# Turning the PSUM banks of the plain blocks by one and making exp(q) one block sooner, in a fused linear-attention and SiLU-MLP kernel

## The chip, the cores and the metric

The kernel runs on one core of a Trainium2 chip. The metric is the device time of a run in microseconds (us), lower is better. A core has five engines that work side by side: PE multiplies matrices and writes its results to PSUM, which has eight banks; ACT evaluates functions such as exp, tanh and silu; DVE and POOL do elementwise work and sums; SP issues most transfers. Only ACT and DVE take results out of PSUM here, so a bank that PE has filled can be filled again only when one of them has read it.

## The reference, cut to what matters

```python
q_s = exp(q - max(q));  q_s = q_s / sum(q_s, over the head dimension)
k_s = exp(k - max(k));  k_s = k_s / sum(k_s, over the sequence)
kv  = k_s^T v                      # per batch and head, 64 x 64
x   = q_s kv                       # reordered to 4608 tokens x 512
out = silu(x @ w_in) @ w_out       # w_in 512 x 2048, w_out 2048 x 512
```

There are 8 batches of 576 rows. The kernel cuts the 4608 tokens into 9 chunks of 512 (0 to 8). It overlaps three things: the first product and the silu of chunk t, the second product of chunk t-1, and the attention of the batch that chunk t+1 needs.

## The kernel before: the parts concerned

Part of the first product is done by seven-multiplication block recursion. In a chunk, half of it comes as 8 **plain blocks** (`p`, one PSUM bank each) and half as 7 **groups** (`g`, two banks each); 14 half-products of the second product (`b`) lie between them. One order is common to chunks 2 to 7:

```python
mix = "pbpbpbpbpbpbpbp", "ggbgbgbgbbgbgb"     # chunk 8 has the second half first
ps_ = [
    lambda t=t, i=i, fb=fb: mm1(t, fb, i < 4 or t + 1 >= B)
    for i, fb in enumerate((0, 8, 1, 9, 2, 10, 3, 11))
]
```

So block 0 is followed by a half-product, and so on, and after block 7 come group 1 and group 2 back to back. The banks of the plain blocks come from a counter (`hb[0]`) taken modulo the length of a ring (`hb[1]`), those of the groups are fixed:

```python
def mm1(t, fb, one=False):
    bank = hb[0] % hb[1]
    hb[0] += 1
    mm1_mm(t, fb, bank, range(NC))                      # 4 matmuls, line 274
    if one:
        nc.scalar.activation(..., func=ACT.Silu, ...)   # line 291: ACT frees the bank
    else:
        mm1_silu(t, fb, bank)      # tanh on ACT (246), then (1 + tanh) * h on DVE (247)

def group(t, i):
    bank = 0 if i in (1, 6, 7, 4) else 2
    ...
    for p in range(4):
        for c in range(2):
            nc.tensor.matmul(out=PS[:, bank + p // 2, ...], ...)    # line 362
```

Tanh and exp come from one ACT table, silu from another. Blocks whose last argument is true use silu; the others use tanh, so that exp(q) can run among them without another table. With tanh the bank is free only after DVE's half. In chunk t the preparation of the next batch is planned at places counted from the chunk's begin `u` (block i is at place 2i):

```python
plan(begin[2], lambda: (hb.__setitem__(0, 3), hb.__setitem__(1, 4)))
plan(begin[3], lambda: hb.__setitem__(0, 1))
...
plan(u + 7 + i, lambda i=i, b=b: exp_q(b, i))
plan(u + 8 + 2 * i, lambda i=i, b=b: (qsum(b, i), qnorm(b, i, nc.gpsimd)))
```

`qsum` is a row sum and a reciprocal on DVE (lines 144 and 148), `qnorm` a multiplication on POOL (line 153). After the last chunk 14 closing half-products (line 460) follow; the first of them writes bank 3.

Three more lines of DVE are named below. Line 480 adds what a product has left in PSUM to a copy that ACT made earlier; the addition called "sa" reads the bank that product 5 writes next. Line 341 adds banks 2 and 3 of a group to a copy that ACT made of banks 0 and 1; group 5 writes bank 2 next. Line 434 makes sums and differences for the second product.

The softmax here doesn't subtract the row's maximum and nothing guards it: scores larger than these inputs give would overflow.

## Time and profile before

| | before |
|---|---|
| time, median of the first 3 runs | 279.14 us (278.73 to 279.38) |
| span of the profiled execution | 277.5 us |
| PE busy | 260.6 us |
| chunk 3 to chunk 4, start of the first group | 28.95 us |
| of it PE waiting ahead of the group | 1.96 us |

The page gives busy time as an average over the span. The last two rows come from the timeline of PE and say more, because a chunk repeats: what is lost in one chunk is lost four times. The lines that carry this are shown in the prediction.

### The profile page before, as it was taken

To read this page: it belongs to the slowest core of one execution; us is meant where nothing else is said; L and a number is where in the kernel's file an instruction comes from. 1 tells how busy PE (TensorE), PEld (TensorE's weight loads), DVE (VectorE), ACT (ScalarE), POOL (GpSimd) and SP (SyncE) were. 2 spreads that over 40 slices of the span, in tenths; PEclk is the share of its full clock that TensorE was granted. 3 is DMA by queue.
4 is the path that set the end of the run, shared out by engine and by line. 5 is a ranking of instruction groups with operands and counts; after the bars stand their busy time and mean duration, and the time that the engine had idled before them with its cause. 6 is when DMAs were issued, how large, how long until landed. Compare 5 with 4: busy or idle time off the path is not lost.

```text
span 277.5 us, 6052 instructions
## 1 busy us (share of the span) xinstructions
PE 260.6 (94%) x2539; PEld 184.7 (67%) x2540; DVE 186.2 (67%) x264; ACT 179.0 (64%) x228; POOL 70.7 (25%) x62
## 2 busy tenths in 40 slices
PE   8799999999999997999799979997999999999993
PEld 3467644456678765876587658764876587886783
DVE  2867797979698749584858495768667237944533
ACT  5667936678866884787568756876677436574310
POOL 1744970900190009000910073005500000000003
PEclk9999999999999999999999999999999999999998
DMA  7999999499369716961696359740406002400534
GB/s 247 322 201 366 260 328 340 119 304 375 108 167 338 165 57 181 328 158 40 191 298 189 73 170 246 241 94 0 87 21 133 0 2 48 106 0 2 123 69 115
DMA packets 35500, 45.88 MB, mean 165 GB/s; under 512 B 16208, under 2 KB 20048, under 8 KB 35472
## 3 DMA queue, kind: packets, MB, share of 16 engines
q1 hardware_dynamic: 29568, 33.69, 43.0%
q0 software_dynamic: 5584, 11.54, 15.9%
q8 instruction: 20, 0.33, 0.5%
q10 hardware_dynamic: 320, 0.26, 0.3%
q14 instruction: 8, 0.07, 0.1%
HBM read 36.70 MB, written 9.44 MB: 166 GB/s over the span
## 4 chain that ended last, share of the span: by engine, by line
PE 71%; DVE 13%; ACT 7%; DMA 4%; issue 2%; SPq 1%; POOL 1%; DVEq 0%
PE PS L460 29%; PE PS L274 16%; PE PS L362 16%; DVE zq L144 5%; DVE GT L247 4%; DMA vt<-in_v_dram 4%; PE PS L398 3%; PE PS L254 3%; ACT eq L108 3%; PE PS L185 2%; ACT L108 2%; PE PS L224 2%; DVE rzq L148 1%; SPq L97 1%; DVE eq L153 1%
## 5 line engine op out<-in xcount | busy, mean ns | idle before, releaser
L274 PE MATMUL PS<-XT,W 128*128 128x512 f16 (+1 forms) x288 | 71.2, 373 | 0.3 <-ACT ow L410 0.3
L460 PEld LDWEIGHTS <-GT 128*128 128x128 f16 x512 | 49.6, 98 | 13.0 <-issue 1.2
L153 POOL TENSOR_TENSOR eq<-eq,rzq 128x1152 bf16<-128x1152 bf16 x13 | 27.5, 2117 | 111.6 <-DVE rzq L148 111.5
L460 PE MATMUL PS<-W,GT 128*128 128x256 f16 x384 | 49.1, 273 | 0.0
L460 PEld LDWEIGHTS <-S 128*128 128x128 f16 x384 | 37.6, 98 | 8.8
L274 PEld LDWEIGHTS <-W 128*128 128x128 f16 x288 | 27.9, 98 | 21.3 <-issue 1.3
L341 DVE TENSOR_TENSOR h<-PS,h 128x1024 f32<-128x1024 f32 x21 | 25.7, 1224 | 24.4 <-ACT h L338 15.3
L247 DVE SCALAR_TENSOR_TENSOR GT<-sg,PS 128x512 f16<-128x512 f32 (+2 forms) x52 | 33.5, 669 | 10.1 <-ACT sg L246 9.8
L246 ACT ACTIVATE sg<-PS 128x512 f32<-128x512 f32 (+2 forms) x52 | 30.1, 596 | 13.4 <-PE PS L274 9.1
L338 ACT COPY h<-PS 128x1024 f32<-128x1024 f32 x21 | 21.3, 1012 | 24.7 <-PE PS L362 24.7
L291 ACT ACTIVATE GT<-PS 128x512 f16<-128x512 f32 x36 | 21.4, 595 | 19.0 <-PE PS L274 18.4
L460 PE MATMUL PS<-T,S 128*128 128x256 f16 x256 | 32.7, 273 | 0.0
L362 PEld LDWEIGHTS <-W 128*128 128x128 f16 x168 | 16.4, 97 | 13.0 <-issue 10.5
L362 PEld LDWEIGHTS <-WS 128*128 128x128 f16 x224 | 21.0, 98 | 4.3 <-issue 1.8
L144 DVE TENSOR_REDUCE zq<-eq 128x18 f32<-128x1152 bf16 x12 | 16.2, 1347 | 11.2 <-ACT eq L108 11.2
L362 PE MATMUL PS<-XS,WS 128*128 128x256 f16 x168 | 21.8, 273 | 0.4 <-ACT h L338 0.4
L362 PE MATMUL PS<-XT,W 128*128 128x256 f16 x112 | 13.7, 272 | 8.5 <-DVE GT L247 7.8
L684 POOL DMA_DIRECT2D out_dram<-ow x4 | 2.2, 550 | 73.4 <-DVE ow L669 73.4
L347 ACT ACTIVATE GT<-h 128x1024 f16<-128x1024 f32 x21 | 20.7, 1052 | 0.0
L111 ACT ACTIVATE ek<-kt 128x1152 bf16<-128x1152 f32 x16 | 18.6, 1164 | 1.8 <-DMA kt<-in_k_dram 1.8
L108 ACT ACTIVATE eq<-qt 128x1152 bf16<-128x1152 f32 x16 | 18.1, 1158 | 2.5 <-DMA qt<-in_q_dram 2.4
L91 POOL CAST vaug<-vt 128x1152 bf16<-128x1152 f32 x12 | 19.4, 1648 | 0.0
(78 smaller groups left out, 337.5 us busy)
## 6 DMA issues: line engine op xcount, KB each, us to landing
out_dram<-ow SPq DMA_DIRECT2D x64, 128.0 KB, 2.4
qt<-in_q_dram SPq DMA_DIRECT2D x12, 576.0 KB, 4.7
kt<-in_k_dram SPq DMA_DIRECT2D x12, 576.0 KB, 7.1
vt<-in_v_dram SPq DMA_DIRECT2D x12, 576.0 KB, 6.1
qt<-in_q_dram POOLq DMA_DIRECT2D x4, 576.0 KB, 13.0
kt<-in_k_dram POOLq DMA_DIRECT2D x4, 576.0 KB, 13.2
vt<-in_v_dram POOLq DMA_DIRECT2D x4, 576.0 KB, 12.5
W<-in_moe_w_out_dram POOLq DMA_DIRECT2D x4, 512.0 KB, 15.2
```

Of the source, the lines that this page charges most:

```text
L108: nc.scalar.activation(out=half(st[b]["eq"], cc), in_=jgd(b, "qt", cc), func=ACT.Exp)
L144: nc.vector.reduce_sum(out=z, in_=e, axis=AX.X)
L153: eng.tensor_tensor(out=e, in0=e, in1=r[:, :, :, None].to_broadcast([128, J, 2, D]), op=ALU.mult)
L246: nc.scalar.activation(out=s, in_=i, func=ACT.Tanh, scale=OS)
L247: nc.vector.scalar_tensor_tensor(out=o, in0=s, scalar=1.0, in1=i, op0=ALU.add, op1=ALU.mult)
L274: nc.tensor.matmul(out=PS[:, bank, o0:TCH], lhsT=W1[:, c, fb * 128:(fb + 1) * 128], rhs=XTS[t % 2][:, c, o0:TCH], start=(c == 0), stop=(c ...
L291: nc.scalar.activation(out=GTS[t % 2][:, fb, 0:TCH], in_=PS[:, bank, :], func=ACT.Silu, scale=1.0 / XS)
L338: nc.scalar.copy(out=H[i], in_=PS[:, 0:2, :].rearrange("p b n -> p (b n)"))
L341: nc.vector.tensor_tensor(out=H[i], in0=PS[:, 2:4, :].rearrange("p b n -> p (b n)"), in1=H[i], op=ALU.add)
L347: nc.scalar.activation(out=group_out(t, f, n), in_=x, func=ACT.Silu, scale=1.0 / XS)
L362: nc.tensor.matmul(out=PS[:, bank + p // 2, (p % 2) * HT:(p % 2 + 1) * HT], lhsT=a[:, c, p * 128:(p + 1) * 128], rhs=bb[:, c, :], start=(i ...
L460: nc.tensor.matmul(out=PS[:, bank, m * HN:(m + 1) * HN], lhsT=a[:, fc, m * 128:(m + 1) * 128], rhs=bb[:, fc, :], start=(first and fc == 0) ...
```

## The change

The intent, as the change states it: the plain blocks' banks are turned by one so that the last two blocks lie in the pair of banks that the groups fill second, and exp(q) is made two blocks sooner, with the second row sum behind a later block. (By the edit it is two places, 7 to 5, which is one block: exp follows block 2's silu where it followed block 3's.)

```diff
-            lambda t=t, i=i, fb=fb: mm1(t, fb, i < 4 or t + 1 >= B)
+            lambda t=t, i=i, fb=fb: mm1(t, fb, i < 3 or t + 1 >= B)
...
-    plan(begin[2], lambda: (hb.__setitem__(0, 3), hb.__setitem__(1, 4)))
-    plan(begin[3], lambda: hb.__setitem__(0, 1))
+    plan(begin[2], lambda: (hb.__setitem__(0, 0), hb.__setitem__(1, 4)))
...
-                plan(u + 7 + i, lambda i=i, b=b: exp_q(b, i))
-                plan(u + 8 + 2 * i, lambda i=i, b=b: (qsum(b, i), qnorm(b, i, nc.gpsimd)))
-                plan(u + 12 + 2 * i, lambda i=i, b=b: vcast(b, i, nc.gpsimd))
+                plan(u + 5 + i, lambda i=i, b=b: exp_q(b, i))
+                plan(u + 6 + 3 * i, lambda i=i, b=b: (qsum(b, i), qnorm(b, i, nc.gpsimd)))
+                plan(u + 10 + 2 * i, lambda i=i, b=b: vcast(b, i, nc.gpsimd))
...
-                    plan(u + 9 + i, lambda i=i, b=b: load(b + 1, "qt", q, i, nc.sync))
+                    plan(u + 7 + i, lambda i=i, b=b: load(b + 1, "qt", q, i, nc.sync))
...
-            plan(u + 14, lambda b=b: q_transpose(b))
+            plan(u + 13, lambda b=b: q_transpose(b))
```

| block | 0 | 1 | 2 | 3 | 4 | 5 | 6 | 7 |
|---|---|---|---|---|---|---|---|---|
| bank before (chunks 3 to 8) | 1 | 2 | 3 | 0 | 1 | 2 | 3 | 0 |
| bank after | 0 | 1 | 2 | 3 | 0 | 1 | 2 | 3 |

## The prediction

> **What bounds the kernel now.** I read the page first. PE is busy for 94% of the span; no other engine passes 67%.
>
> ```profile
> PE 260.6 (94%) x2539; PEld 184.7 (67%) x2540; DVE 186.2 (67%) x264; ACT 179.0 (64%) x228; POOL 70.7 (25%) x62
> ...
> PE 71%; DVE 13%; ACT 7%; DMA 4%; issue 2%; SPq 1%; POOL 1%; DVEq 0%
> ```
>
> PE carries 71% of the chain that ended last, but DVE and ACT stand in it with 20%: there PE stood still. The waits of PE alone say where:
>
> ```profile
> PE PS L362 <- DVE GT L247: 7.8, 5, 1.8
> ...
> PE PS L362 <- ACT GT L291: 0.7, 1, 0.7
> ```
>
> L362 is the first product of a group, L247 the DVE half of a block's silu. The wait comes once in each token chunk of 512 that has a group behind plain blocks (chunks 2 to 7): about 1.8 us in chunks 3 to 6, 0.58 in chunk 2, 0.7 in chunk 7, where silu is one ACT instruction. Everything else PE waits for in the steady part is 0.4 us. The chain around one wait (chunk 4; start, length, what):
>
> ```profile
> 126.64 0.88 PE PS L274 x4
> 127.51 0.02 issue
> 127.53 0.04 ACT GT L291
> 127.58 0.57 issue
> 128.15 1.14 ACT L108
> 129.29 0.16 issue
> 129.44 1.17 ACT eq L108
> 130.62 0.02 issue
> 130.64 1.36 DVE zq L144
> 132.00 0.03 issue
> 132.03 0.02 DVEq L148
> 132.05 0.04 issue
> 132.10 0.27 DVE rzq L148
> 132.36 0.54 DVE GT L247
> 132.91 1.27 DVE zq L144
> 134.17 0.02 issue
> 134.20 0.27 DVE rzq L148
> 134.46 1.74 DVE GT L247 x3
> 136.21 0.04 issue
> 136.25 1.91 PE PS L362 x16
> ```
>
> Read it from the top: block 3 ends on PE, ACT does its silu, loads another table, makes exp(q); DVE makes two row sums, each ahead of silu halves that are waiting, and only then frees the last block's bank. PE's last block, in the timeline, starts at 133.42 and takes 0.87, so PE is free at 134.29 and starts the group at 136.25: **1.96 us idle per chunk**. The chunk lasts 28.95 us (107.30 to 136.25 between group starts), so its PE work is 26.99.
>
> The banks explain why it waits for the *last* block. Before, from chunk 3 on, blocks 0..7 lie in banks 1,2,3,0,1,2,3,0; group 1 fills banks 0 and 1, group 2 banks 2 and 3. The first matmul of group 1 goes to bank 0, which holds block 7. In chunk 2 they lie in 3,0,1,2,3,0,1,2, which is why that wait is short.
>
> **What the Trainium skill says.** "PSUM — Partial Sum Buffer", in its summary for kernel authors, says to guard PSUM by bank and to read one bank while the matmul targets another. The trace agrees: group 1 starts 0.04 us after the last L247 in its bank. "ScalarE: Activation LUTs", section "What ACT_TABLE_LOAD costs", gives about 1283 ns for the load plus about 1380 ns of drain. The trace has five loads of 1.28 us at L108; no such drain is visible (silu ends 128.13, load 128.15, exp 129.44). The same page lists exp and tanh in one set: the trace has no load between exp and tanh here. "SBUF — State Buffer", section "Who interferes with whom", says that DVE instructions with two SBUF inputs contend with GpSimd reads. The trace agrees: the L434 subtraction that follows the last silu takes 1.69 us beside POOL's work in chunk 4, and 1.22 in chunk 7 without it.
>
> **The change part by part.** The order of instructions per engine shows: PE, POOL and SP keep their order. ACT keeps its 173 rows; its table load and two exps move ahead by one silu, and block 3 becomes tanh. DVE gets five more rows (one L247 in each of chunks 2 to 6): about 0.6 x 5 = 3 us of DVE work, on an engine with a third idle. The first row sum comes ahead of block 3's half, the second behind block 4's; the addition "sa" moves between.
>
> *Turned banks.* Blocks now lie in 0,1,2,3,0,1,2,3. Group 1 needs blocks 4 and 5, group 2 blocks 6 and 7. The order's waits show four on DVE, one per bank, each four matmuls (half of 0.87 = 0.44 us) apart. So the group starts at once and needs the last bank only 1.31 us later.
>
> *exp(q) sooner.* Block 2's silu ends at 126.40 (start 125.80, 0.60). I move the ACT chain by 1.73, the distance of two blocks' silus (127.53 - 125.80):
> - exp 127.71 to 129.93 for both; tanh of blocks 3, 4, 5 at 129.84, 130.31 and 131.00 (5 by its matmuls' end); tanh 6 at 132.74 and 7 at 134.48, both still bound by PE; 7 ends 135.08.
> - DVE: first sum at 128.91, reciprocal 130.37, block 3's half 130.55, "sa" 131.09, block 4 at 131.7, second sum 132.25 (1.38 to its reciprocal), block 5 at 133.8 to 134.43, block 6 to 135.0, block 7 from 135.12 to 135.75.
>
> Put together, PE free at 134.29: bank 0 is free (block 4 ended about 132.3), bank 1 asked for at 134.73 (free 134.47), bank 2 at 135.16 (free 135.04), bank 3 at 135.60, free at 135.79. **Left over: 0.19 us instead of 1.96, a gain of 1.77**, four times: 7.1 us.
>
> *Chunk 2.* Before: PE free 77.30, the product after the two groups at 80.09; two groups take 1.74, so 1.05 idle. After, as above, 0.19. Gain 0.86.
>
> *Chunk 7* (no exp, all silu on ACT): free 221.11, started 221.95. Block 7's silu ends at 221.91; its bank is now asked for only at 222.42. Gain 0.84.
>
> *Chunk 8, a loss.* Here groups come first, and the closing products follow the plain blocks at once: the first goes to bank 3. Before, bank 3 held block 6 and nothing waited. Now it holds block 7, whose silu runs 261.07 to 261.67. The products started at 260.87; they will start at about 261.71. Loss 0.84, in a run of products that is the chain to the end.
>
> Sum: 7.1 + 0.86 + 0.84 - 0.84 = 7.9 us; 279.14 - 7.9 = **271.2 us**, 2.8% less. Each part alone, by the same clockwork: banks alone gain about 1.3 a chunk (block 7 still at 136.20, its bank needed last), earlier exp alone 0.46 (136.25 to 135.79).
>
> **The rivals.**
> (1) *A new wait takes its place inside the group.* PE gains 1.77 us but DVE only 0.45, so DVE runs 1.3 us later against PE. I checked each consumer: product 5 overwrites the bank that "sa" reads: needed 132.54, ready 131.78 (margin 0.76). The L434 result for product 7: needed 137.96, ready 137.35 (0.6). Group 5 overwrites bank 2, read by the L341 addition: needed 138.84, ready about 138.5 (0.3). The first is paid by moving "sa" behind a 1.36 us row sum. For it: margins are small, and POOL slows DVE. Against it: before, DVE idled 0.56 and 2.20 us in that stretch, so it catches up. If group 5 waits 0.3 in five chunks: 272.7.
> (2) *The preparation of q, k and v becomes the bound:* POOL's normalisations and casts, the transpose, exp(k). POOL starts its second normalisation about 0.5 earlier while PE runs 1.77 earlier; casts end about 139.4, k-v products want them at 140.68 (margin 1.2). The transposed q is wanted at 143.3 and lands near 140.7 (136.1 + 4.6). Little speaks for it; it would give back up to 1 us a chunk, 276.
> (3) *The gain is only that of the earlier exp* because group 1 waits as a whole for its pair and the next: then 0.63 stays per chunk and the result is 273.5. The waits per bank speak against it.
> (4) *The end's loss is hidden:* then 270.4. The products there run without a gap to the last, so I don't expect it.
>
> **How the range and the chances follow.** The sum of the measured times gives 271.2. Rival 1 makes it 272.7, rival 4 270.4; the three runs before spread 0.65 us. I take 270.2 to 273.0. Two per cent would be 273.56, which needs 2.4 us of the 7.9 to fail in the recurring chunks; I give 0.9 to faster, 0.09 to same, 0.01 to slower.
>
> **What would show it.** Right: the waits of PE for L247 at L362 shrink from 7.8 to about 1 us in all, in pieces near 0.2; chunks of the steady part last about 27.2 us; exp starts about 1.73 us sooner against its chunk; DVE has five more L247 and ACT five fewer L291; a new wait of about 0.7 to 0.8 us of the closing products (L460) for ACT's L291. Wrong: a wait at L362 for L341, at L460 for L434 or L480, or at the k-v products for POOL or ACT; or group 1 still starting late after block 7.

## The result, and the profile after

The changed kernel took 271.18 us (median of 4, 270.92 to 271.64) against 278.94 (median of 4) for the kernel before, 7.76 us less. The ratio is 0.9723, 95% interval 0.9702 to 0.9744. A ratio here is the mean time of one kernel's fast runs over that of the other's fast runs of the same rounds, so it is not quite the ratio of the two medians.

On the page of the changed kernel (the profiler's summary of one execution), the busy times and the chain by engine. The chain is the work that ended last, followed back at each step to what released it:

```profile
PE 260.4 (97%) x2540; PEld 184.6 (69%) x2540; DVE 190.6 (71%) x269; ACT 180.1 (67%) x228; POOL 71.1 (26%) x62
...
PE 71%; DVE 15%; ACT 8%; issue 3%; DMA 1%; POOL 1%; DVEq 0%
```

PE does the same 260 us of work in a shorter span, and DVE has five more instructions. The chain still passes through DVE and ACT with about the same share. That alone would look as if nothing had changed: the chain follows whatever released PE last, and DVE still releases the group last, however short the wait. How long PE stood still is in the list of its waits (engine, line, waited for: us in total, times, longest), of which these are the ones of the chunks and of the end:

```profile
PE PS L460 <- ACT GT L291: 0.7, 1, 0.7
PE PS L362 <- ACT h L338: 0.4, 1, 0.4
```

The 7.8 us of line 362 waiting for line 247 and the 0.7 waiting for line 291 are gone from the list, and one new wait of 0.7 us is there: the closing products, as predicted. The list is not the whole truth, though. Here is PE's timeline around the groups of chunk 4 before (start, length, engine, line; idle before in brackets):

```profile
133.42 1.03 PE L274 MATMUL PS<-XT,W 128*128 128x512 f16 x4
136.25 1.91 PE L362 MATMUL PS<-XT,W 128*128 128x256 f16 x16 [1.80 <-DVE GT L247]
137.99 1.04 PE L460 MATMUL PS<-T,S 128*128 128x256 f16 x8
```

And the same place after:

```profile
130.40 1.03 PE L274 MATMUL PS<-XT,W 128*128 128x512 f16 x4
131.26 2.17 PE L362 MATMUL PS<-XT,W 128*128 128x256 f16 x16
133.26 1.04 PE L460 MATMUL PS<-T,S 128*128 128x256 f16 x8
```

After the change the group starts 0.86 us after block 7, which is the time of the block itself: at once. But from its start to the next product are 2.00 us, where 1.74 are work. The missing 0.26 us is a wait inside the group, and only the start-to-start distance shows it. The chain of waits of the changed kernel at this place (start, length, what) says for what:

```profile
130.90 0.56 DVE GT L247
131.46 0.01 issue
131.46 0.61 ACT sg L246
132.07 0.02 issue
132.09 0.70 DVE GT L247
132.79 0.04 issue
132.83 0.60 PE PS L362 x4
```

The last four of the group's 16 matmuls, those in bank 3, start 0.04 us after DVE's half of block 7, and that half follows block 7's own tanh. The row sums are no longer directly ahead of it. The chain names DVE as what released that tanh, but it was PE. What ended on DVE at 131.46 is block 5's half, and in chunk 4 before, block 7's tanh began (134.48) while block 5's half was still running (134.38 to 135.01). In both traces the tanh starts 1.06 us after block 7's first matmul (130.40 to 131.46, 133.42 to 134.48).

At the end, PE's timeline from the last plain block, first before, then after:

```profile
260.01 1.03 PE L274 MATMUL PS<-XT,W 128*128 128x512 f16 x4
260.87 3.66 PE L460 MATMUL PS<-W,GT 128*128 128x256 f16 x32
```

```profile
251.02 1.03 PE L274 MATMUL PS<-XT,W 128*128 128x512 f16 x4
252.73 3.65 PE L460 MATMUL PS<-W,GT 128*128 128x256 f16 x32 [0.69 <-ACT GT L291]
```

From block to product 0.86 us have become 1.71: a loss of 0.85 that the change itself brought in.

Where the time came from, by the starts in the timelines of the two profiled executions:

| stretch | before | after | gain |
|---|---|---|---|
| start to block 1 of chunk 2 | 66.01 | 65.50 | 0.51, code unchanged |
| chunk 2, block 1 to the product behind the groups | 14.08 | 13.28 | 0.80 |
| chunks 3 to 6, block 0 of chunk 3 to block 0 of chunk 7 | 115.78 | 108.94 | 6.84 (4 x 1.71) |
| chunk 7, block 0 to group 1 of chunk 8 | 26.98 | 26.14 | 0.84 |
| chunk 8, group 1 to the closing products | 25.80 | 26.65 | -0.85 |

The parts that the change touches sum to 7.63 us; the runs show 7.76. The two spans differ by 8.1, because the profiled execution of the changed kernel also had the shorter start.

### The profile page after: what moved, and what is told of

Its sections match the earlier page's. It is cut to its first block, busy times and chain, and to the rows that moved or that the text cites. A ratio compares the mean times of both kernels' runs of the same rounds, so it can differ in the third digit from the quotient of the medians.

```text
span 269.4 us, 6058 instructions
## 1 busy us (share of the span) xinstructions
PE 260.4 (97%) x2540; PEld 184.6 (69%) x2540; DVE 190.6 (71%) x269; ACT 180.1 (67%) x228; POOL 71.1 (26%) x62
## 4 chain that ended last, share of the span: by engine, by line
PE 71%; DVE 15%; ACT 8%; issue 3%; DMA 1%; POOL 1%; DVEq 0%
PE PS L460 29%; PE PS L274 16%; PE PS L362 14%; DVE zq L144 5%; DVE GT L247 4%; PE PS L398 3%; PE PS L254 3%; ACT eq L108 3%; PE PS L224 2%; PE PS L185 2%; DVE eq L153 2%; ACT sg L246 2%; ACT L108 2%; DMA qt<-in_q_dram 1%; DVE ow L480 1%
## 5 line engine op out<-in xcount | busy, mean ns | idle before, releaser
L247 DVE SCALAR_TENSOR_TENSOR GT<-sg,PS 128x512 f16<-128x512 f32 (+2 forms) x57 | 37.4, 671 | 10.4 <-ACT sg L246 9.7
L246 ACT ACTIVATE sg<-PS 128x512 f32<-128x512 f32 (+2 forms) x57 | 33.1, 595 | 16.9 <-PE PS L274 8.1
L291 ACT ACTIVATE GT<-PS 128x512 f16<-128x512 f32 x31 | 18.5, 595 | 13.3 <-PE PS L274 12.7
L254 PE MATMUL PS<-XT,W 128*128 128x288 f16 x128 | 16.5, 286 | 0.7 <-DVE GT L247 0.4
```

The source lines that it names most:

```text
L246: nc.scalar.activation(out=s, in_=i, func=ACT.Tanh, scale=OS)
L247: nc.vector.scalar_tensor_tensor(out=o, in0=s, scalar=1.0, in1=i, op0=ALU.add, op1=ALU.mult)
L254: nc.tensor.matmul(out=PS[:, 2 * (fb % 3) + n, 0:S // 2], lhsT=W1[:, c, fb * 128:(fb + 1) * 128], rhs=XTS[0][:, c, n * (S // 2):(n + 1) * ...
```

## The experiments

Eight kernels ran, all with correct results. The first four ran on one chip, the other four on another. The kernel before ran again (medians 279.01 and 279.11), the changed kernel did not; so a time is compared with the changed kernel's by the ratios to the kernel before and by the length of a chunk. `Chunk` below is the distance from block 7 of one chunk to block 7 of the next in the steady part: 28.95 us before, 27.24 after.

### The two halves of the change, each alone

Banks alone (the kernel before with the bank counters of the change and nothing else of it):

```diff
-    plan(begin[2], lambda: (hb.__setitem__(0, 3), hb.__setitem__(1, 4)))
-    plan(begin[3], lambda: hb.__setitem__(0, 1))
+    plan(begin[2], lambda: (hb.__setitem__(0, 0), hb.__setitem__(1, 4)))
```

> Only the banks turned; exp(q) and the row sums where they were before. Theory (each bank of the group waits for its own block, the last one 1.31 us after the group starts): the silu halves still end where they did, so about 0.65 us of idle stays per chunk with a row sum instead of 1.96; chunks 3 to 6 gain 1.3 each, chunk 2 0.4, chunk 7 0.84, chunk 8 loses 0.85: about 273.3 us, a gain of 5.6. Rival (the group waits as a whole for the last block): no gain in chunks 2 to 6, about 279.

Measured: 273.61 us (median of 5), ratio to before 0.9799, chunk 27.64. The timeline of PE in chunk 4 shows the wait *inside* the group:

```profile
131.55 1.03 PE L274 MATMUL PS<-XT,W 128*128 128x512 f16 x4
132.41 0.60 PE L362 MATMUL PS<-XT,W 128*128 128x256 f16 x4
133.19 1.79 PE L362 MATMUL PS<-XT,W 128*128 128x256 f16 x12 [0.18 <-DVE GT L247]
134.81 1.04 PE L460 MATMUL PS<-T,S 128*128 128x256 f16 x8
```

The group starts at once, does its four matmuls in bank 0, and only then waits for the next bank. From start to next product are 2.40 us, so 0.66 is lost (0.65 was expected): about half of it ahead of the second bank (0.78 us from start to start where four matmuls take 0.44) and the rest within the other twelve.

Exp alone (the changed kernel with the old banks; block 3's tanh, the casts, the load of q and the transpose keep their new places too, and no run takes these apart):

```diff
-    plan(begin[2], lambda: (hb.__setitem__(0, 0), hb.__setitem__(1, 4)))
+    plan(begin[2], lambda: (hb.__setitem__(0, 3), hb.__setitem__(1, 4)))
+    plan(begin[3], lambda: hb.__setitem__(0, 1))
```

> Only exp(q) and the row sums moved; the banks as before. Theory: the group waits for block 7 in bank 0, which is freed 0.39 us sooner than before (its own tanh and DVE half bound it, not the row sums): gain 0.39 in each of chunks 3 to 6, 0.36 in chunk 2, nothing in 7 and 8: about 277.0 us, a gain of 1.9. Rival (the earlier exp is the main part, the wait was the exp and row-sum chain): exp moves by 1.73 us per chunk, so a gain of 1.7 x 5 = 8, about 271.

Measured: 276.93 us (median of 6), ratio 0.9931, chunk 28.55. The same place of the timeline:

```profile
131.69 1.03 PE L274 MATMUL PS<-XT,W 128*128 128x512 f16 x4
134.12 1.91 PE L362 MATMUL PS<-XT,W 128*128 128x256 f16 x16 [1.41 <-DVE GT L247]
```

Exp moved by 1.73 us and the wait shrank by 0.4, because the next limit, block 7's own tanh and DVE half, stands right behind. So most of the gain is the banks', about 5.4 us, and exp adds about 2; by ratios, 2.0% and 0.7% of 279. The two add: exp takes 0.40 us off a chunk with the old banks (28.95 to 28.55) and 0.40 with the new (27.64 to 27.24).

### Per bank or as a whole

The changed kernel with blocks 6 and 7 exchanged in banks 2 and 3, in chunks 2 to 6:

```diff
         bank = hb[0] % hb[1]
         hb[0] += 1
+        if 2 <= t < B - 1 and fb in (3, 11):
+            bank = 5 - bank
```

> The changed kernel, but in chunks 2 to 6 block 6 lies in bank 3 and block 7 in bank 2. Theory (waits per bank): the last-freed bank is asked for 0.44 us sooner, the wait in the group grows from 0.26 to about 0.7 us, five times: about 273.4 us. Rival (the second group waits for its pair of banks as a whole): no change, 271.2.

Measured: 273.78 us (median of 4), ratio 0.9804, chunk 27.68, which is 0.44 longer than 27.24. Both blocks end as before and lie in the same pair; only the bank that is asked for earlier holds the later block. The second group now stops ahead of its first matmul (two lines are inserted, so line 362 is 364 here):

```profile
132.55 1.04 PE L364 MATMUL PS<-XT,W 128*128 128x256 f16 x8
134.12 1.03 PE L364 MATMUL PS<-XT,W 128*128 128x256 f16 x8 [0.53 <-DVE GT L247]
```

The wait is per bank, and four matmuls of 0.11 us, the lead of one bank over the next, can be seen in the time.

### The loss at the end

The changed kernel with the bank counter set to 1 ahead of chunk 8:

```diff
     plan(begin[2], lambda: (hb.__setitem__(0, 0), hb.__setitem__(1, 4)))
+    plan(begin[NCH - 1], lambda: hb.__setitem__(0, 1))
```

> The changed kernel, but in chunk 8 the banks start at 1 again, so that the last block lies in bank 0 and the first closing product finds bank 3 with block 6. Theory: the 0.85 us that chunk 8 lost comes back and nothing else changes: about 270.3 us. Rival (the closing products wait for the last block's data, not for its bank): no change, 271.2.

Measured: 270.36 us (median of 4), ratio 0.9691 against 0.9723, 0.9 us of 279. The closing products start 0.86 us after the last block again (250.68 to 251.54), and their wait for line 291 is gone from the list. It was the bank, not the data.

### Where the second row sum stands

Two places sooner:

```diff
-                plan(u + 6 + 3 * i, lambda i=i, b=b: (qsum(b, i), qnorm(b, i, nc.gpsimd)))
+                plan(u + 6 + 1 * i, lambda i=i, b=b: (qsum(b, i), qnorm(b, i, nc.gpsimd)))
```

> The changed kernel, but the second row sum two places sooner, so that both row sums lie ahead of the addition 'sa' and of block 4's silu half. Theory: 'sa' frees the bank of product 5 about 1.56 us later than in the changed kernel, where the margin was 0.76: product 5 waits about 0.8 us in each of chunks 2 to 6 and all behind it moves, about 275.2 us. Rival (DVE's order does not matter as long as its work ends before the group): no change, 271.2.

Measured: 275.66 us (median of 6), ratio 0.9875, chunk 28.10, or 0.86 longer. The group's own loss stays as it was; PE now stops at product 5, whose bank the addition "sa" (line 480) reads:

```profile
131.56 1.03 PE L274 MATMUL PS<-XT,W 128*128 128x512 f16 x4
133.29 1.03 PE L460 MATMUL PS<-T,S 128*128 128x256 f16 x8 [0.70 <-DVE ow L480]
```

One place sooner, between "sa" and block 4's half:

```diff
-                plan(u + 6 + 3 * i, lambda i=i, b=b: (qsum(b, i), qnorm(b, i, nc.gpsimd)))
+                plan(u + 6 + 2 * i, lambda i=i, b=b: (qsum(b, i), qnorm(b, i, nc.gpsimd)))
```

> The changed kernel, but the second row sum one place sooner: behind 'sa', ahead of block 4's silu half. Theory: nothing waits for block 4's bank before 134.3 of chunk 4's clock and it is free about 133.9, so no change, 271.2 us, and the group takes as long as in the changed kernel. Rival (that the second sum lies behind two silu halves matters by itself): slower by 0.5 us a chunk, 273.7.

Measured: 271.47 us (median of 4), ratio 0.9719, chunk 27.28. No difference that the runs can tell. The trace shows where the 0.04 us of a chunk arise (times of chunk 4): line 434 takes 2.04 us here, so the addition of line 341 ends at 135.54 (134.33 + 1.21), and group 5 starts at 135.60, 0.92 us after the product ahead of it where 0.87 is usual. So what matters is that the second sum stands behind "sa"; that it stands behind one more silu half is worth those 0.04.

### What is left

The 0.26 us inside the group can be covered if other work stands between the two groups. The changed kernel with a half-product moved there:

```diff
-        mix = "pbpbpbpbpbpbpbp", "ggbgbgbgbbgbgb"
+        mix = "pbpbpbpbpbpbpbp", "gbggbgbgbbgbgb"
```

> The changed kernel, but in chunks 2 to 7 the second half of product 5 is done between groups 1 and 2. Theory: the bank of block 7 is asked for 0.87 us later, so the 0.26 us left in each of chunks 2 to 6 is covered; about 1.3 us less, 269.9 us. Rival (DVE follows: the addition that group 5 waits for ends at about 138.5 of chunk 4's clock, and group 5 would start at 138.65): the wait moves to group 5 and the time stays 271.2.

Measured: 269.98 us (median of 5), ratio 0.9667, chunk 26.98. That is the 26.99 of pure PE work that the prediction had worked out from the chunk before. The timeline of PE in chunk 4:

```profile
130.07 1.03 PE L274 MATMUL PS<-XT,W 128*128 128x512 f16 x4
130.93 1.04 PE L362 MATMUL PS<-XT,W 128*128 128x256 f16 x8
131.81 1.04 PE L460 MATMUL PS<-T,S 128*128 128x256 f16 x8
132.68 1.04 PE L362 MATMUL PS<-XT,W 128*128 128x256 f16 x8
133.55 1.04 PE L362 MATMUL PS<-XS,WS 128*128 128x256 f16 x8
```

Each piece starts 0.86 to 0.88 us after the one before: no gap, and none at group 5 either (start 135.30, 0.87 after the product ahead of it).

Both repairs, this one and the banks of chunk 8:

```diff
-        mix = "pbpbpbpbpbpbpbp", "ggbgbgbgbbgbgb"
+        mix = "pbpbpbpbpbpbpbp", "gbggbgbgbbgbgb"
...
+    plan(begin[NCH - 1], lambda: hb.__setitem__(0, 1))
```

> The changed kernel with both repairs: the banks of chunk 8 started at 1, and product 5's second half between groups 1 and 2. Theory: the two are in different chunks and add: 271.2 - 0.85 - 1.3 = 269.0 us. Rival (the wait moves to group 5): 270.3, as with the banks of chunk 8 alone.

Measured: 269.48 us (median of 4, 269.38 to 269.62), ratio 0.9652, the fastest of all, beating both kernels of the change. Against the changed kernel it gains 2.0 us by ratios where 2.15 were expected. Its trace shows both repairs (chunk 26.98, and from the last block to the closing products 0.87 us), so what is missing of the expected 269.0 is not in them. Its interval, 0.9634 to 0.9669, overlaps that of the kernel with the first repair alone, 0.9648 to 0.9685, so these two runs alone would not prove that the repairs add. The stretch up to block 1 of chunk 2, which no experiment changes, took between 65.03 and 66.79 us in the ten profiles, and differences of half a microsecond between medians could come from there; that was not tested.

## Why the prediction was right

It said 271.2 us and 271.18 was measured. That they agree to 0.02 is luck: the gain was put 0.1 to 0.3 us too high (7.9; the runs gave 7.76, the terms in the trace 7.63), and the kernel before, from which it was taken off, came out 0.2 us faster over four runs (278.94) than over the three known then (279.14). A sum can be right by errors that cancel, so point by point:

- **The wait is for a bank, and the last block's bank decides.** Right: banks alone gave 0.66 us of idle for 1.96, and the exchange of two blocks within their pair cost 0.44 a chunk.
- **0.19 us left per chunk.** Measured 0.26, so the gain per chunk was 1.71 and not 1.77. The term that was mis-sized is DVE's half of block 7: I took 0.63, which the first half of a run of halves takes in the trace before (132.28, 0.63), but when it comes alone after a wait it takes 0.70 (132.09 to 132.79). The same term made the earlier exp alone worth 0.40 a chunk and not 0.46.
- **Chunk 2: 0.86.** Measured 0.80, by the same term.
- **Chunk 7: +0.84; chunk 8: -0.84.** Measured +0.84 and -0.85. Undoing the turn in chunk 8 won the loss back.
- **Exp and the row sums.** On chunk 4's clock (after plus 3.02, the shift of block 7) exp starts at 127.71, the first sum at 128.91, "sa" at 131.09, block 7's half ends at 135.81; predicted were 127.71, 128.91, 131.09 and 135.75.
- **Rival 1, a new wait.** It did not come. DVE's line 434 did not take 1.69 but 1.54 us this time. On the changed kernel's own clock the addition for group 5 ended at 135.37, and group 5 started at 135.88, straight after the product ahead of it: a margin of 0.5 where 0.3 was expected. It is a real limit all the same: with line 434 at 2.04 us (the sum one place sooner) group 5 did wait, 0.04 us. That the margin of "sa" was real and small is shown by moving the sum: with 1.56 us more ahead of it PE lost 0.86 per chunk (0.8 predicted for it).
- **Rival 2, the preparation as the bound,** did not come: PE's list has no wait of the k-v products in the chunks.
- **Rival 3, the group waiting as a whole,** fell with the group's start straight after block 7 and with the exchange of the two blocks. Its sum was not thought through: 0.63 left per chunk fits a second group that waits for its own pair (135.16 to 135.79). If group 1 had waited for both pairs, as the text has it, 1.5 us would have stayed (134.29 to 135.79).
- **Rival 4, a hidden loss at the end,** fell with the trace and with the repaired banks.
- **What I said the profile would show was partly wrong.** I expected the list to keep about 1 us for line 362 in pieces of 0.2. It has none. The pieces are there, but the list leaves them out, for the reason told in the last section. The other signs came: chunks of 27.24 us, exp 1.73 us sooner, line 247 at 57 instructions where there were 52 and line 291 at 31 where there were 36, and 0.7 us of the closing products.

The sum of the measured terms is 4 x 1.71 + 0.80 + 0.84 - 0.85 = 7.63 where I had 7.9; the runs gave 7.76.

## What to carry to other kernels

When work B takes over a ring of buffers from work A, lay the ring out so that A's last buffers are those that B fills last; it costs no instruction, and here it gave more than moving the whole chain ahead of the wait. Then look at every other place that follows the ring: the same turn put the last block into the first bank of the closing products. When a chain is moved sooner, ask first what stands right behind it: 1.73 us sooner were worth 0.4 a chunk, with the old banks and with the new.

## What the Trainium skill lacked or had wrong

- "PSUM — Partial Sum Buffer", summary for kernel authors, says to read a bank other than the one the matmul targets, and to guard by bank. It has no word on the order in which a ring of banks is handed from one phase to the next; here that order alone was worth about 5.4 us of 279 (banks alone, 273.61).
- "ScalarE: Activation LUTs", "What ACT_TABLE_LOAD costs", adds about 1380 ns of drain to the load's 1283. The load agrees (1.28 us). No run here shows the drain as time: silu ends 123.38, load 123.39, exp 124.69 in the changed kernel, 1.31 us for the whole switch.
- "SBUF — State Buffer", "Who interferes with whom", says that a DVE instruction with two SBUF inputs contends with a GpSimd (POOL) instruction that reads SBUF. The page also says that the second to issue is blocked until the first finishes, but it has no measured time for such a pair. One subtraction of line 434 (128x2048, f16) took 1.21 to 1.23 us with POOL idle. Where a multiplication or cast of POOL had begun before it, it took 1.34 to 2.13 us, and in all 82 such cases of the ten traces it ended 1.07 to 1.08 us after that POOL instruction did. So its length is set by what is left of POOL's instruction, as the page has it: in chunk 4 POOL's multiplication ended 0.61 us after the subtraction began before the change (1.69) and 0.46 after it (1.54).
- "Perfetto Trace Analysis", "Tensor Engine Instruction", says that the end of a matmul is estimated. What follows for reading waits is missing: the idle time shown is about 0.16 us less than the time lost from start to start (1.80 for 1.96, 0.69 for 0.85, 0.53 for 0.70), because the modelled end of the matmul ahead reaches that far past the moment when the next could start: a plain block is shown 1.03 us long, and the next work can start 0.86 after its start. Short waits vanish: the 0.26 in each group stands in no list.
